# Router pacing, unread matmuls and an earlier weight split in an attention and mixture-of-experts kernel

## The chip, the cores and the metric

The kernel runs on one core of a Trainium2 chip. The metric is the device time of one execution in microseconds. Five engines work side by side, each with its own instruction queue: TensorE (PE, matmuls and transposes), VectorE (DVE), ScalarE (ACT), GpSimd (POOL) and SyncE (SP, which issues most DMA transfers).

## The reference, cut to what matters

```python
# 4 x 8 heads, 512 local tokens (window 32) and 32 global ones, head size 64
x = attention(q_l, k_l, v_l, q_g, k_g, v_g)       # 4 x 544 = 2176 tokens x 512
logits = x @ w_gate                                # 8 experts
order = argsort(-logits.flatten())                 # best pair first
for idx in order:
    tok, e = idx // 8, idx % 8
    if assigned[tok] >= 0 or counts[e] >= 272:
        continue
    assigned[tok] = e; counts[e] += 1
for e in range(8):
    out[assigned == e] = relu(x[assigned == e] @ w1[e]) @ w2[e]
g = out @ w_gate2                                  # gated layer, 512 -> 1536 -> 512
return (silu(g) * (out @ w_val)) @ w_out
```

The capacity of an expert is 272 tokens. A token goes to its best expert that still has room, and the order over all pairs decides who gets the room.

## The kernel before, in words

**Attention** comes first. Beside it a converter (class `Convert`) rewrites the weights of the last, gated layer into a format of 32-bit words: for each half tile it loads raw data (L110), takes a magnitude on ScalarE (L116), builds the word in three VectorE instructions (L122 to L124) and stores it (L128). `LD` says how many rounds a load runs ahead of the magnitude, `RAWB` how many raw buffers there are. Thirty of the 36 half tiles are converted in attention, the last six later, a little at every tick.

**The router** fills the experts one at a time (`Router.phase`). A phase finds the score limit of one expert in six steps: VectorE compares all scores with 32 limits (L678, `cmp`), TensorE counts by 17 short matmuls (L685), VectorE picks the bracket (L688 to L690) and keeps the upper bound (L671 to L674). Then come the number of the expert (`eis`, L704, which SyncE reads to load that expert's weights), the mask, the prefix sum (L717, L718), a one-hot comparison (L734 or L739) with a small product beside it (`h3` at L728, `rh` at L729), and the index matmuls (L743). For expert 0, `W` in these lines is GpSimd, for all others it is VectorE. `Router.after` takes the assigned tokens out (its count matmul is L767).

**The experts** run in four groups of two. Expert k's 272 tokens are gathered by three indirect DMAs (`fetch`, L884), transposed on TensorE (L902) in blocks of 128, 128 and 16, and split into a rounded part `xH` (ScalarE, L904) and a remainder `xL` (VectorE, L905); every product is three matmuls, H by H, H by L and L by H. The weights, in tiles of 512 KB, are split in the same way by `parts` (L983 on ScalarE, L984 on VectorE). `moe` runs h(f), the first layer, and y(f), the second; `gated` runs the gated layer of one expert of the group; four such blocks of expert 0 (`early`) come between expert 0 and expert 1. Banks b0 to b5 are in pairs: `hb` for h, `yb` for y, and gated blocks go round the three pairs.

**The order of the work** is written by one generator, `background`, which hands out the router's instructions step by step. After each piece of 12 matmuls the main program calls `tick`, and a step that yields n is followed by n ticks until the next. While expert k is fetched, a countdown (`GW`, `GL`) runs in the same steps before its transposes are issued. `hurry` changes the yields. `wait_for(k)` drives the generator without any ticks until expert k's transposed tokens are there; in that case the transposes go to the banks b0 to b2, otherwise to one bank, `xbank`. `pump` splits a tile if it was asked for at least `LAG` ticks ago, and at the latest when the product needs it; `load` issues the DMAs of the next tiles.

Of the kernel before, what the change touches and what calls it, by code (L numbers as in the profile page):

```python
# [14 lines left out]
ALU = mybir.AluOpType  # L15
# [49 lines left out]
CV0, CV1 = 3, 6  # L65
QB = 8
PL = 2
RAWB, CB, FB, LD = 5, 3, 4, 3
NC = 30
EN = 36  # L70
UO, LW = 0, 39
# [470 lines left out]
class Router:  # L542
# [110 lines left out]
    def phase(s, n):  # L653
        nc, V, K, b = s.nc, s.nc.vector, s.K, s.bank
# [4 lines left out]
        if not last:  # L659
            lo = s.gmin  # L660
            KS, NR = KN[0]
            cmp, ge = s.cmp[:, :, 0:KS], s.ge[:, 0:KS]
            V.tensor_scalar(s.d, s.hi, s.gmin, 1e-26, op0=ALU.subtract, op1=ALU.max)
            Td = s.Td[:, 0:KS * NR].rearrange("p (r k) -> p r k", k=KS)
            V.tensor_scalar(Td, s.io[0], s.d, None, op0=ALU.mult)
            def step(k):

                return Td[:, k, 1:2]
            def bound(k):

                V.tensor_scalar(s.m1, k1, KS - 1.5, 1e38, op0=ALU.is_ge, op1=ALU.mult)  # L671
                V.tensor_scalar(s.k2, k1, 1.0, None, op0=ALU.add)
                V.scalar_tensor_tensor(s.cd, s.k2, step(k), old, op0=ALU.mult, op1=ALU.add)
                V.scalar_tensor_tensor(s.hi, s.cd, s.m1, s.hi, op0=ALU.max, op1=ALU.min)  # L674
            parts = ((0, 9), (9, NCH)) if n == 0 else ((0, NCH),)
            for k in range(NR):
                for c0, c1 in parts:
                    V.scalar_tensor_tensor(cmp[:, c0:c1], Td[:, k, None, :].to_broadcast([128, c1 - c0, KS]), lo,  # L678
                                           s.v[:, c0:c1, None].to_broadcast([128, c1 - c0, KS]), op0=ALU.add, op1=ALU.is_le)
                if k:  # L680
                    bound(k - 1)
                yield TA, RF
                cnt = b[:, 0:KS]
                for c in range(NCH):
                    nc.tensor.matmul(cnt, s.ohr[:, c].rearrange("p r e -> p (r e)"), cmp[:, c, :], start=c == 0, stop=c == NCH - 1)  # L685

                k1, new = s.k1[k % 2], s.lo2[k % 2]
                V.tensor_scalar(ge, cnt, s.nd, -1.0, op0=ALU.is_ge, op1=ALU.add, accum_out=s.ke)  # L688
                V.tensor_reduce(k1, s.ke.to_broadcast([128, 32]), axis=AX.X, op=ALU.max, apply_transpose=True)
                V.scalar_tensor_tensor(new, k1, step(k), lo, op0=ALU.mult, op1=ALU.add)  # L690
                old, lo = lo, new

            V.scalar_tensor_tensor(s.ew, s.ke, k1, s.w8p, op0=ALU.is_ge, op1=ALU.mult)
            V.tensor_reduce(s.em, s.ew.to_broadcast([128, 32]), axis=AX.X, op=ALU.max, apply_transpose=True)
            bound(NR - 1)
            V.tensor_scalar(s.G, s.v, lo, None, op0=ALU.is_ge)
            V.tensor_scalar(s.A, s.v, s.hi, None, op0=ALU.is_ge)
            V.tensor_tensor(s.G, s.G, s.A, op=ALU.subtract)
        else:
            V.scalar_tensor_tensor(s.e8, s.pen, OUTV / 2, s.w8, op0=ALU.is_ge, op1=ALU.mult)  # L700
            V.tensor_reduce(s.em, s.e8, axis=AX.X, op=ALU.max)
            V.tensor_scalar(s.A, s.v, OUTV / 2, None, op0=ALU.is_ge)
            V.memset(s.G, 0.0)
        V.tensor_scalar(s.eis[n], s.em, -1.0, 8.0, op0=ALU.mult, op1=ALU.add)  # L704
        s.known = n
        yield 1, 0.0

# [8 lines left out]
        p = b[:, 320:354]  # L716
# [5 lines left out]
        W = nc.gpsimd if n == 0 else V  # L722
# [2 lines left out]
            V.tensor_copy(s.lob[:, 0:NCH], s.lo)  # L725
        V.tensor_tensor(s.hb, s.pp[:, None, :].to_broadcast([128, 4, NCH]), s.thr[:, :, None].to_broadcast([128, 4, NCH]), op=ALU.is_ge)
        yield 1, 0.0
        W.tensor_tensor(s.h3, s.hb[:, 0:3], s.hb[:, 1:4], op=ALU.subtract)  # L728
        W.tensor_tensor(s.rh, s.h3.rearrange("p k c -> p c k")[:, :, :, None].to_broadcast([128, NCH, 3, 2]),  # L729
                        s.rid[:, :, None, :].to_broadcast([128, NCH, 3, 2]), op=ALU.mult)  # L730
        for c0, c1 in ((0, 8), (8, NCH + 1)):
# [3 lines left out]
            else:  # L735

                x = slice(c0, min(c1, NCH))
# [36 lines left out]
GW, GL = 6, 12  # L774

EARLY = (4, 5)
CV2 = 0.4
LA0 = 3
MO = 1
# [2 lines left out]
WB, LOOK, RAWS, LAG = 6, 4, 4, 4  # L782
class Ffn:
# [39 lines left out]
    def background(s):  # L823


        pend, now = [], None
        for k in range(E):
            for y in s.steps(k):
                yield s.hurry(k, y)
                if pend and now is None and s.moes >= pend[0] - 1:  # L830
                    now = s.fetch(pend.pop(0))
                    left = next(now)
                    yield 1, 0.0
                elif now is not None:
                    left -= y[0]
                    if left <= 0:
                        x = next(now)
                        if isinstance(x, int):
                            left = x
                        else:  # L840
                            yield x
                            yield from now
                            now = None
            if k < E:
                s.done_phase = k
            pend.append(k)
            if now is None and s.moes >= pend[0] - 1:
                now = s.fetch(pend.pop(0))
                left = next(now)
                yield 1, 0.0  # L850
        while pend or now is not None:
            if now is not None:
                x = left
                while isinstance(x, int):
                    for _ in range(x):
                        yield 1, 0.0
                    x = next(now)
                yield x
                yield from now
                now = None  # L860
            elif s.moes >= pend[0] - 1:
                now = s.fetch(pend.pop(0))
                left = next(now)
            else:
                yield 1, 0.0
# [6 lines left out]
    def hurry(s, k, y):  # L872

        if k == 1:
            return (0 if y[0] == 1 else TA, y[1])

        return (y[0] + (y[0] > 1 and k > 1 and not s.cv.finished), y[1])

    def fetch(s, k):

# [4 lines left out]
                                         in_offset=bass.IndirectOffsetOnAxis(ap=s.R.idx[k][0:n, blk:blk + 1], axis=0))  # L885
        if k == 0:

            yield 2
            for m in range(2):
                s.pump(m, 0)  # L890
                yield (1, 3)[m]
        else:
            yield GW if k == 1 else GL
        xH = s.pool.tile([128, 4, TE], F32R, name="xH", bufs=2)
        xL = s.pool.tile([128, 4, TE], F32R, name="xL", bufs=2)
        s.xT[k] = (xH, xL)
        for blk, n in enumerate((128, 128, 16)):
# [7 lines left out]
            nc.vector.tensor_tensor(xL[:, :, sl], p, xH[:, :, sl].bitcast(F32), op=ALU.subtract)  # L905
            yield 0, 0.0
            if not s.waiting:
                yield 1, 0.0
        s.ready.add(k)

    def convert(s, n):
# [105 lines left out]
    def wait_for(s, k):  # L1017
        s.waiting = True
        while k not in s.ready:
            next(s.bgen)  # L1020
            s.load()
        s.waiting = False

    def moe(s, k, e):
# [144 lines left out]
    def run(s, ext):  # L1169
# [3 lines left out]
        for _ in s.bgen:  # L1173
            if s.R.known == 0:
                while s.nd < LA0:
                    s.dma(s.nd); s.asked[s.nd] = -1; s.nd += 1
            if s.done_phase == 0:
                break
        s.wait_for(0)
# [57 lines left out]
```

## Time and profile before

| | |
|---|---|
| median of 3 runs | 941.58 us (940.79 to 944.29) |
| profiled execution | 935.68 us, span 933.9 us |
| mean granted TensorE clock | 0.959 |
| TensorE busy | 855.0 us (92% of the span) |
| VectorE busy | 598.8 us (64%) |
| ScalarE busy | 398.0 us (43%) |

The span goes from the first to the last instruction of the profiled execution; busy times are sums over the instructions of an engine, and TensorE's are modelled from its pipelined matmuls.

### The profile page before, as it was taken

Reading aid. Unit: us, or ns where it says so; the run is one execution under the profiler, and the core shown is the slowest. Engines: PE = TensorE matmul, PEld = TensorE weight load, DVE = VectorE, ACT = ScalarE, POOL = GpSimd, SP = SyncE. Lnnn points to the kernel's source line nnn. Section 1 sums busy time; section 2 is a strip of 40 time slices with the busy share of each in tenths; the row PEclk is TensorE's granted clock in tenths of the full one; section 3 lists DMA queues with packets and bytes.
Section 4 is the critical chain, followed back from the end, with each engine's and each line's share of the span. In section 5 each row is a group of like instructions: output and inputs, shape, how many; then the busy total and the mean of one; then the engine's idle time right before and its main releaser. Section 6 shows DMA issues by size and latency. Waiting matters only on the chain.

```text
span 933.9 us, 19229 instructions
## 1 busy us (share of the span) xinstructions
PE 855.0 (92%) x7567; PEld 791.7 (85%) x7567; DVE 598.8 (64%) x1486; ACT 398.0 (43%) x827; POOL 111.9 (12%) x189
## 2 busy tenths in 40 slices
PE   6999998638879888999999989999999999999997
PEld 6888887428878887889989888899999889999985
DVE  3688778787889876658888776575545335644410
ACT  4888788313444332324433322245444234443300
POOL 5343321010100000110100100210100020000002
PEclk9999999858989999999999999999999999999999
DMA  7998988242546522434532221365422345522101
GB/s 176 251 268 234 277 261 266 101 160 68 184 157 212 192 73 90 138 102 147 181 116 92 69 71 66 126 215 159 137 91 90 92 137 178 156 72 92 46 1 56
DMA packets 109962, 130.72 MB, mean 140 GB/s; under 512 B 57456, under 2 KB 75120, under 8 KB 109872
## 3 DMA queue, kind: packets, MB, share of 16 engines
q1 hardware_dynamic: 106432, 120.45, 42.1%
q0 software_dynamic: 2896, 8.92, 2.7%
q8 instruction: 59, 0.97, 0.4%
q14 instruction: 31, 0.25, 0.1%
q10 hardware_dynamic: 544, 0.13, 0.1%
HBM read 111.12 MB, written 18.35 MB: 139 GB/s over the span
## 4 chain that ended last, share of the span: by engine, by line
PE 50%; issue 21%; DVE 20%; ACT 4%; DMA 2%; POOL 1%; SPq 0%; POOLq 0%; DVEq 0%; ACTq 0%
PE b L1013 9%; PE b L1015 8%; PE b L1014 8%; DVE wHL L984 4%; PE b L1130 4%; PE b L1131 4%; PE b L1132 4%; DVE r_cmp L678 2%; PE s L303 2%; PE tr L323 2%; PE o L334 2%; DVE b L1078 1%; ACT dH L1079 1%; PE o L339 1%; DMA cv_raw<-moe_w_val 1%
## 5 line engine op out<-in xcount | busy, mean ns | idle before, releaser
L1013 PE MATMUL b<-yH,wHL 128*128 128x272 f32 x768 | 228.7, 298 | 0.0
L1015 PE MATMUL b<-yH,wHL 128*128 128x272 f32 x768 | 224.9, 293 | 0.0
L1014 PE MATMUL b<-yL,wHL 128*128 128x272 f32 x768 | 224.5, 292 | 0.0
L984 DVE TENSOR_TENSOR wHL<-raw,wHL 128x1024 fp32r<-128x1024 f32 x140 | 169.0, 1225 | 45.2 <-ACT wHL L983 44.7
L983 ACT CAST wHL<-raw 128x1024 fp32r<-128x1024 f32 x140 | 143.3, 1047 | 77.9 <-PE b L1132 42.4
L1013 PEld LDWEIGHTS b<-yH,wHL 128*128 128x128 f32 x768 | 148.1, 193 | 3.1 <-issue 3.0
L1014 PEld LDWEIGHTS b<-yL,wHL 128*128 128x128 f32 x768 | 148.6, 194 | 0.2 <-DVE yL L1063 0.2
L1015 PEld LDWEIGHTS b<-yH,wHL 128*128 128x128 f32 x768 | 148.2, 193 | 0.0
L1079 ACT CAST dH<-b 128x272 fp32r<-128x272 f32 x96 | 37.1, 387 | 182.7 <-DVE b L1078 182.7
L1078 DVE TENSOR_TENSOR b<-b,si 128x272 f32<-128x272 f32 x96 | 42.8, 446 | 57.7 <-PE b L1015 57.5
L1013 PE MATMUL b<-dH,wHL 128*128 128x272 f32 x256 | 76.7, 299 | 1.0 <-ACT wHL L983 1.0
L1013 PE MATMUL b<-xH,wHL 128*128 128x272 f32 x252 | 75.3, 299 | 2.2 <-ACT xH L904 1.3
L1015 PE MATMUL b<-dH,wHL 128*128 128x272 f32 x256 | 75.2, 294 | 2.3 <-DVE wHL L984 2.3
L1130 PE MATMUL b<-wHL,dH 128*128 128x512 f32 x192 | 76.3, 397 | 0.0
L1014 PE MATMUL b<-dL,wHL 128*128 128x272 f32 x256 | 74.9, 292 | 1.5 <-DVE dL L1041 1.5
L1131 PE MATMUL b<-wHL,dL 128*128 128x512 f32 x192 | 75.9, 395 | 0.0
L1132 PE MATMUL b<-wHL,dH 128*128 128x512 f32 x192 | 75.9, 395 | 0.0
L1014 PE MATMUL b<-xL,wHL 128*128 128x272 f32 x252 | 73.9, 293 | 0.3 <-DVE xL L905 0.3
L1015 PE MATMUL b<-xH,wHL 128*128 128x272 f32 x252 | 74.0, 294 | 0.0
L1080 DVE TENSOR_TENSOR dL<-b,dH 128x272 fp32r<-128x272 f32 x96 | 42.4, 442 | 43.6 <-ACT dH L1079 43.1
L1040 ACT ACTIVATE dH<-b 128x272 fp32r<-128x272 f32 x64 | 25.5, 398 | 103.7 <-PE b L1015 98.8
L884 POOL DMA_INDIRECT xg<-xd,r_idx x24 | 26.0, 1085 | 264.0 <-DVE b L1078 74.8
(237 smaller groups left out, 1609.5 us busy)
## 6 DMA issues: line engine op xcount, KB each, us to landing
raw<-wd SPq DMA_DIRECT2D x76, 512.0 KB, 3.7
raw<-moe_w SPq DMA_DIRECT2D x64, 512.0 KB, 3.8
wd<-cv_f SPq DMA_DIRECT2D x36, 256.0 KB, 4.8
cv_raw<-moe_w_gate SPq DMA_DIRECT2D x12, 512.0 KB, 6.3
cv_raw<-moe_w_val SPq DMA_DIRECT2D x12, 512.0 KB, 4.4
cv_raw<-moe_w_out SPq DMA_DIRECT2D x12, 512.0 KB, 6.9
xd<-xt SPq DMA_DIRECT2D x16, 256.0 KB, 5.9
st<-k_l SPq DMA_DIRECT2D x28, 128.0 KB, 5.3
```

Source lines behind the costliest of these rows:

```text
L884: nc.gpsimd.indirect_dma_start(out=xg[0:n, blk, :], out_offset=None, in_=s.K.xd[:, :], in_offset=bass.IndirectOffsetOnAxis(ap=s.R.idx[k][0 ...
L983: nc.scalar.copy(w[:, 0], raw)
L984: nc.vector.tensor_tensor(w[:, 1], raw, w[:, 0].bitcast(F32), op=ALU.subtract)
L1013: nc.tensor.matmul(out, wH, xH, start=start, stop=False)
L1014: nc.tensor.matmul(out, wH, xL, start=False, stop=False)
L1015: nc.tensor.matmul(out, wL, xH, start=False, stop=stop)
L1078: nc.vector.tensor_tensor(b, b, si, op=ALU.mult)
L1079: nc.scalar.copy(dH[:, f, :], b)
L1080: nc.vector.tensor_tensor(dL[:, f, :], b, dH[:, f, :].bitcast(F32), op=ALU.subtract)
L1130: nc.tensor.matmul(ob[i], dh, H[:, f % 2, :], start=f == 0, stop=False)
L1131: nc.tensor.matmul(ob[i], dl, H[:, f % 2, :], start=False, stop=False)
L1132: nc.tensor.matmul(ob[i], dh, L[:, f % 2, :], start=False, stop=f == 11)
```

## The change

The converter's loads go one round further ahead, with seven buffers instead of five. The expert number is written before the bounds and masks. `h3` of expert 0 moves from GpSimd to VectorE. Router steps of more than one tick take one tick more for all experts from the third on, also after the converter has ended. A new function `warm` issues matmuls whose result is never read, at four places. The first three weight tiles are split while expert 0's rows are gathered. While TensorE waits for an expert's tokens, their transposes are issued without the countdown; blocks that aren't waited for are two ticks apart instead of one. While expert 0 is waited for, no further loads are issued. The four early blocks stay as they are.

```diff
-RAWB, CB, FB, LD = 5, 3, 4, 3
+RAWB, CB, FB, LD = 7, 3, 4, 4
...
             V.tensor_reduce(s.em, s.ew.to_broadcast([128, 32]), axis=AX.X, op=ALU.max, apply_transpose=True)
+            V.tensor_scalar(s.eis[n], s.em, -1.0, 8.0, op0=ALU.mult, op1=ALU.add)
             bound(NR - 1)
...
-        V.tensor_scalar(s.eis[n], s.em, -1.0, 8.0, op0=ALU.mult, op1=ALU.add)
+            V.tensor_scalar(s.eis[n], s.em, -1.0, 8.0, op0=ALU.mult, op1=ALU.add)
...
-        W.tensor_tensor(s.h3, s.hb[:, 0:3], s.hb[:, 1:4], op=ALU.subtract)
+        V.tensor_tensor(s.h3, s.hb[:, 0:3], s.hb[:, 1:4], op=ALU.subtract)
...
+W0, W1, W2, W3 = 4, 6, 8, 2
...
-                    if left <= 0:
+
+                    if left <= 0 or s.waiting and k > 1:
                         x = next(now)
...
-        return (y[0] + (y[0] > 1 and k > 1 and not s.cv.finished), y[1])
+        return (y[0] + (y[0] > 1 and k > 1), y[1])
+
+    def warm(s, n):
+
+        x = s.R.iota2.rearrange("p w c -> p (w c)")[:, 0:512]
+        for _ in range(n):
+            s.nc.tensor.matmul(s.B[s.hb[1]], s.K.identb, x, start=True, stop=True)
...
+            s.warm(W0)
             yield 2
-            for m in range(2):
-                s.pump(m, 0)
-                yield (1, 3)[m]
+            for m in range(3):
+                s.parts(m); s.np += 1
+                yield 1
+            s.warm(W1)
         else:
+            if s.waiting:
+                s.warm(W2)
             yield GW if k == 1 else GL
+            if s.waiting:
+                s.warm(W3)
...
             if not s.waiting:
-                yield 1, 0.0
+                yield 2, 0.0
         s.ready.add(k)
...
         while k not in s.ready:
             next(s.bgen)
-            s.load()
+            if k:
+
+                s.load()
...
-                    s.dma(s.nd); s.asked[s.nd] = -1; s.nd += 1
+                    s.dma(s.nd); s.asked[s.nd] = -LAG; s.nd += 1
```

## Rows read from the trace of the kernel before

**Rows 1.** The page's view of the span in 40 slices: TensorE's granted clock.

```profile
PEclk9999999858989999999999999999999999999999
```

**Rows 2.** Busy time by stretch: stretch, its length, each engine's busy us, clock, DMA share, GB/s.

```profile
core 0: us, PE busy (x) PEld busy (x) DVE busy (x) ACT busy (x) POOL busy (x), PEclk, DMA share, GB/s
...
176.00:209.00 33.00, 9.96 (x156) 8.16 (x156) 27.85 (x122) 3.47 (x5) 4.55 (x5) 0.53 0.33 113
209.00:249.00 40.00, 33.94 (x301) 32.55 (x297) 32.35 (x105) 12.79 (x20) 2.38 (x2) 0.84 0.35 106
...
302.00:337.00 35.00, 29.77 (x251) 29.42 (x250) 29.49 (x73) 13.04 (x28) 2.77 (x3) 1.00 0.54 172
337.00:377.00 40.00, 34.84 (x325) 33.85 (x325) 28.06 (x94) 13.21 (x27) 0.59 (x1) 0.90 0.18 62
...
418.00:470.00 52.00, 50.09 (x457) 48.69 (x456) 45.90 (x124) 23.38 (x38) 6.01 (x5) 1.00 0.50 155
470.00:515.00 45.00, 42.44 (x425) 41.44 (x425) 36.08 (x108) 16.12 (x35) 0.00 (x0) 1.00 0.31 98
515.00:570.00 55.00, 48.56 (x433) 47.07 (x432) 39.49 (x131) 16.56 (x37) 3.37 (x4) 0.94 0.22 68
...
395.00:400.00 5.00, 5.00 (x23) 3.85 (x23) 2.82 (x11) 0.27 (x2) 0.00 (x0) 1.00 0.30 106
```

**Rows 3.** TensorE's waits, 302 to 570 us: us in total, times, longest.

```profile
PE rbank L685 <- DVE r_cmp L678: 7.9, 5, 3.3
PE xbank L902 <- DVE xL L905: 6.5, 4, 2.4
PE rbank L717 <- DVE r_Mb L712: 3.3, 3, 2.2
PE rbank L767 <- DVE r_acc L759: 2.4, 1, 2.4
```

**Rows 4.** VectorE's groups by line, 302 to 606: busy us, mean ns, idle before.

```profile
L984 DVE TENSOR_TENSOR wHL<-raw,wHL 128x1024 fp32r<-128x1024 f32 x53 | 64.3, 1228 | 9.4 <-ACT wHL L983 8.9 <-issue 0.5
L1078 DVE TENSOR_TENSOR b<-b,si 128x272 f32<-128x272 f32 x44 | 19.5, 443 | 7.9 <-PE b L1015 7.8
L1080 DVE TENSOR_TENSOR dL<-b,dH 128x272 fp32r<-128x272 f32 x44 | 19.4, 442 | 20.0 <-ACT dH L1079 19.5 <-issue 0.5
...
L728 DVE TENSOR_TENSOR r_h<-r_hb 128x51 f32<-128x51 f32 x6 | 1.2, 205 | 0.0
```

**Rows 5.** ScalarE's waits in attention, 0 to 176 us.

```profile
ACT cv_a L116 <- DMA cv_raw<-moe_w_val: 5.6, 4, 2.2
```

**Rows 6.** Timeline, 193 to 220 us: start, us, instruction, idle before it.

```profile
193.98 0.15 DVE L704 TENSOR_SCALAR r_ei<-r_em 128x1 int32<-128x1 f32 x1
...
196.07 0.59 POOL L728 TENSOR_TENSOR r_h<-r_hb 128x51 f32<-128x51 f32 x1 [40.93 <-DVE r_hb L726]
...
205.74 1.97 PE L902 MATMUL b<-identf,xg 128*128 128x128 f32 x8 [5.22 <-DMA xg<-xd,r_idx]
207.91 0.60 PE L902 MATMUL b<-identf,xg 16*128 16x16 f32 x4 [0.21 <-DMA xg<-xd,r_idx]
...
216.97 0.39 PE L1013 MATMUL b<-dH,wHL 128*128 128x272 f32 x1 [0.99 <-ACT wHL L983]
...
219.77 0.59 PE L1015 MATMUL b<-dH,wHL 128*128 128x272 f32 x1 [2.28 <-DVE wHL L984]
```

**Rows 7.** Timeline where the early blocks end and expert 1 begins.

```profile
263.58 2.36 DVE L984 TENSOR_TENSOR wHL<-raw,wHL 128x1024 fp32r<-128x1024 f32 x2 [0.50 <-ACT wHL L983]
...
267.30 0.61 PE L685 MATMUL rbank<-r_cmp,r_ohr 128*128 128x32 bf16 x17 [4.66 <-DVE r_cmp L678]
...
268.06 0.44 DVE L1080 TENSOR_TENSOR dL<-b,dH 128x272 fp32r<-128x272 f32 x1 [0.45 <-ACT dH L1079]
...
269.17 0.59 PE L1013 MATMUL b<-xH,wHL 128*128 128x272 f32 x1 [1.26 <-ACT xH L904]
```

**Rows 8.** Timeline of VectorE: first and last of the nine instructions of a step.

```profile
344.05 0.24 DVE L688 TENSOR_SCALAR_CACHE_REDUCE r_ge<-rbank,r_nd 128x32 bf16<-128x32 f32 x1
...
346.04 0.22 DVE L674 SCALAR_TENSOR_TENSOR r_hi<-r_cd,r_m,r_hi 128x1 f32<-128x1 f32 x1
```

## The prediction

> **What bounds the kernel now.** I read the page's line of TensorE's granted clock over the span first: each digit is a fortieth of the span, 23.3 us, in tenths of full speed, and it falls in four of them between 163 and 280 us [rows 1]. So the question for any edit is where TensorE still stands or runs slowly. The view of busy time by stretch answers it: from 176 to 209 TensorE has 10 us of work in 33 at a clock of 0.53, because VectorE finds the first expert's tokens alone; from 209 to 249 (expert 0) it has 33.9 us in 40 at clock 0.84; from 302 to 377 and 418 to 570 it still loses time in pieces [rows 2].
>
> For the last part, lost time in a stretch is idle time plus (1 - clock) times the stretch: 5.2 us in 302-337, 5.2 + 4.0 in 337-377, 1.9 in 418-470, 2.6 in 470-515, 6.4 + 3.3 in 515-570, in all 28.6 us. The list of waits says for what: the router's counting matmuls waiting for VectorE's comparison (7.9 us), the token transposes waiting for VectorE to empty their one bank (6.5), the prefix-sum matmul (3.3), the count matmul L767 (2.4) [rows 3]. All are VectorE. It isn't full there (28.1 of 40 us in 337-377 [rows 2]), so it is its queue's order that hurts: what the next matmul needs stands behind splits of 1.23 us each [rows 4].
>
> **The change part by part.** Sums are made against the profiled execution, 935.7 us with a span of 933.9. The three timed runs have a median of 941.6, 5.9 us above it; I carry each difference over to that median.
>
> *Attention (RAWB 7, LD 4).* Each converter load is issued one round earlier, with two more buffers; bytes are the same. ScalarE waited for these loads 5.6 us in four places [rows 5], with other engines still at work. Best case all of it and some queueing behind it, -5; worst +1, since the first round puts one more 512 KB load into the queue, ahead of the next heads' loads. I take -2.
>
> *Up to the first expert's matmul.* The expert number is written before seven small instructions instead of after them: it was done at 193.98 and would be about 1.0 us sooner, and the three weight loads with it. h3 leaves GpSimd (0.59 us) for VectorE, where the same shape takes 0.21 [rows 4, 6]: the index matmuls could start about 0.4 us sooner, but VectorE's two large comparisons start 0.2 later. Against that, the third tile's split adds 1.23 us to VectorE's queue ahead of the first comparison and of xL. Ten unread matmuls of 512 columns cost about 0.22 us each at full clock (23 in 5.0 us, last row of [rows 2]), double that at half: 4.3 us at most, in gaps where TensorE stood anyway; the last of these gaps is 5.2 us, until the gathered rows land at 205.7 [rows 6]. If that cover were gone they would cost up to 4.3 us. I take 0, bounds -2.5 and +1.5.
>
> Here a rule of the Trainium skill bears on it ("TensorE: Matmul & The Clock Gate", Part 1: the throttled clock is the resting state, and activity lifts it). The trace agrees: the clock is 0.53 where TensorE has 10 us of work in 33 [rows 2]. By that rule the unread matmuls would let the transposes (2.6 us at half clock [rows 6]) and what follows run at full clock, and the term would be its lower bound of -2.5; I keep 0, since VectorE, late by one split, would take it back.
>
> *Expert 0.* In the kernel before, the third tile was split only when y(0) asked for it: TensorE stood 0.99 and 2.28 us and fell to half clock behind it [rows 6]. Now it is split before the expert starts. The stretch 209-249 loses 6.1 us idle and 6.4 to the clock; but VectorE has 32.4 us of work in it [rows 2], all of it still to do, so at most 40 - 32.4 = 7.6 can go. I take -5, bounds -7.5 and -2. The skipped load() calls while waiting for expert 0 cost nothing: SyncE has no other transfer between those loads.
>
> *Early blocks and the boundary to expert 1.* By a count of the program's ticks, the countdown of the second fetch is already spent when the early blocks end, so the new "waiting and k > 1" condition fires where the old one did: the transposes keep their place in the queue. Two things do change. One split fewer stands in VectorE's queue at the boundary, where two took from 263.58 to 265.94 [rows 7]: -1.2. And two unread matmuls go ahead of the transposes, into bank hb[1]. The fourth early block uses that same bank, and its last reader is dL L1080, which ended at 268.50 [rows 7]. So twelve transposes, which stood ahead of the router matmul of 267.30 and ran beside VectorE's backlog, now wait for that backlog's end. Before, expert 1 started 0.67 us behind this dL (269.17); now follow 0.9 us of unread matmuls, 2.6 us of transposes at the slow clock (1.97 + 0.60 for the first expert's [rows 6]) and the last copy, about 4 us: +3.3. Expert 1 then starts with a warmer clock, -1. Together +1, bounds -2 and +3.5.
>
> A second rule speaks against this part of the change ("TensorE: Matmul & The Clock Gate", Part 2: matmuls stay in program order, only weight loads are pulled ahead). The trace agrees: expert 1's first matmul stands behind a router matmul that waits 4.66 us [rows 7].
>
> *Group 0 and group 1: router paced.* Steps of more than one tick now take one more, also after the converter is done; it ends at about tick 50, in the middle of group 0. A tick is 12 matmuls of about 0.12 us (29.8 us for 251 in 302-337, at full clock [rows 2]), some 1.5 us. One router step is nine VectorE instructions from 344.05 to 346.26, 2.2 us [rows 8]. A gated block adds b, dL and the hole between them (0.44 + 0.44 + 20.0/44 = 1.34 us in two ticks [rows 4]), and splits, two in eight ticks, 0.3 us a tick. Before, a step every two ticks: 1.1 + 0.67 + 0.3 = 2.1 us of VectorE in 1.5 of TensorE; after, every three: 1.7 in 1.5, and six ticks without steps while the transposes go through, two ticks apart instead of one, so that the copies of a block have 3 us. Three pairs of banks cover a lag of some 6 us. So most waits of [rows 3] should go, with the clock's dips behind them, but not L767's 2.4, which comes before the pacing differs. Group 0 (14.4 of the 28.6 us): -10, bounds -4 and -13. Group 1 and its experts (14.2): -7, bounds -3 and -10.
>
> *What is late next.* By the same count, expert 3's tokens are known two ticks into expert 2 instead of ten ticks ahead of it, and its fetch countdown has not run out when expert 2 ends: its three transposes come in the gap. Their banks are those whose yL is written last, then copies follow, some 3.3 us until the first two matmuls can go; 2.2 of these are transposes and a router step that TensorE had to do anyway. Expert 5 is caught with its smallest block alone. And the sixth phase now runs beside experts 4 and 5, which had no router work. I take +1.5 + 0.5 + 0.5 = +2.5, bounds 0 and +8 (expert 3 as bad as expert 1).
>
> The sum: -2 + 0 - 5 + 1 - 10 - 7 + 2.5 = **-20.5**, a profiled time of 915 and a median of **921 us**.
>
> **The rivals.** *Half of it:* VectorE stays the limit in the groups with 1.7 us per tick against 1.5, so pacing gives half (-8.5 for -17), and the load lead gives nothing: 0 + 0 - 5 + 1 - 8.5 + 2.5 = -10, 932 us. For it: the figure of 1.7; against: VectorE's 12 us of idle time in 337-377.
>
> *All of it:* attention -4, first matmul -2, expert 0 -7, boundary -1, groups -23, late parts +3: -34, 908 us. For it: every wait named is one of order; against: VectorE's 32.4 us in expert 0.
>
> *Slower:* VectorE's lag is not removed but carried to the boundaries. The groups then give nothing, and experts 3 and 5 each wait as expert 1 did, 4.66 us for the comparison and 1.26 for the copies [rows 7], with some 2 us of slow clock after it, about 8 us each: -2 + 0 - 5 + 1 + 0 + 16 = +10, 952 us. It decides once the two waits take over 6 us more than the groups give. For it: expert 3's fetch is surely late; against: its rows have 12 ticks, 18 us, to land, and router work in expert 2 falls.
>
> *The named part does nothing:* the condition for the second expert's transposes has no effect. That is part of my forecast.
>
> **How the numbers follow.** Two runs of this kernel tell about 0.5% apart, 4.7 us. Forecast 0.55, half of it 0.20, all of it 0.16, slower 0.09. The likeliest has its own range of 913 to 930; from "all of it" to a little over "half of it" the range is 907 to 937. Faster by over 0.5%: all of the first and third, 0.71, and most of "half of it", 0.13, makes 0.84; within 0.5%: 0.09, the rest of "half of it" and 0.02 of the slower case; slower: 0.07.
>
> **What would show it.** Right: no idle time of over 1 us before y(0) of expert 0; the waits of router matmuls and xbank transposes in groups 0 and 1 under 6 us together; clock at or near 1.00 there. At expert 1 the unread matmuls start only when dL has ended, and the transposes behind them. At expert 3 the transposes write banks b, not xbank. Wrong: attention ending more than 3 us later, expert 3 or 5 waiting over 5 us, or the lost time of 302 to 570 still above 20 us.

## The result and the profile after

The changed kernel takes 907.98 us (median of 4 runs, 906.74 to 909.42) where the kernel before takes 941.18 (4 runs): ratio 0.9647, 95% interval 0.9612 to 0.9681, or 33 us less. The forecast was 921, the range 907 to 937. The sign held, and the range held by 1 us; the gain is 13 us larger than forecast, at the end that the rival "all of it" had given (908).

The profiled execution of the changed kernel took 909.42 us with a span of 907.6. Line numbers have moved by up to 18 (L984 is now L1000, L902 is L918, L1013 to L1015 are L1029 to L1031, L1080 is L1098; the unread matmul is L887).

First the page's line of TensorE's granted clock, which answers to [rows 1]:

```profile
PEclk9999999857889999999999999999999999999999
```

The dips between 160 and 270 us are still there and no shallower. What has gone is idle time after 300 us, with the smaller dips behind it (0.90 and 0.94 in [rows 2]). The view of busy time by stretch, for stretches as in [rows 2] (its columns are the same):

```profile
177.00:211.00 34.00, 14.84 (x159) 9.63 (x159) 29.21 (x123) 4.37 (x6) 4.64 (x4) 0.52 0.35 112
211.00:249.00 38.00, 34.00 (x320) 32.95 (x317) 34.08 (x108) 13.69 (x22) 3.85 (x3) 0.85 0.44 151
302.00:337.00 35.00, 33.03 (x278) 32.79 (x278) 28.98 (x72) 13.77 (x28) 2.76 (x3) 1.00 0.52 166
337.00:372.00 35.00, 34.69 (x328) 33.18 (x328) 26.72 (x73) 15.66 (x32) 1.20 (x2) 1.00 0.32 105
371.00:429.00 58.00, 58.00 (x385) 51.05 (x384) 38.16 (x97) 18.84 (x28) 10.95 (x12) 1.00 0.45 146
429.00:459.00 30.00, 29.27 (x294) 28.25 (x293) 25.95 (x78) 13.62 (x24) 0.00 (x0) 1.00 0.48 147
459.00:514.00 55.00, 55.00 (x508) 54.45 (x506) 41.70 (x107) 22.56 (x47) 3.38 (x3) 1.00 0.29 95
514.00:560.00 46.00, 45.87 (x324) 40.78 (x321) 29.76 (x91) 12.57 (x23) 4.90 (x5) 1.00 0.32 105
```

From 302 to 560 us the clock is 1.00 everywhere, and TensorE is idle 2.0 us in the first of these stretches, 0.7 at expert 3's start (429 to 459) and 0.4 in the others together. Its waits from 285 to 570 us, which answer to [rows 3] and begin 17 us earlier:

```profile
PE rbank L768 <- DVE r_acc L760: 2.0, 1, 2.0
PE b L1030 <- DVE dL L1059: 1.5, 1, 1.5
PE b L1029 <- DVE xL L921: 0.7, 1, 0.7
PE rbank L685 <- DVE r_cmp L678: 0.5, 2, 0.3
```

The waits for the comparison, the transposes' bank and the prefix sum, 17.7 us in [rows 3], have become 0.5 (0.2 from 302 us on). VectorE's instructions have not become shorter (groups by line, 302 to 606 us, as [rows 4]): the hole ahead of dL is still 20.0 us.

```profile
L1000 DVE TENSOR_TENSOR wHL<-raw,wHL 128x1024 fp32r<-128x1024 f32 x62 | 74.4, 1220 | 7.6 <-ACT wHL L999 7.5
...
L1098 DVE TENSOR_TENSOR dL<-b,dH 128x272 fp32r<-128x272 f32 x44 | 19.4, 442 | 20.0 <-ACT dH L1097 20.0
```

The timeline of TensorE up to expert 0's second layer, as [rows 6]:

```profile
200.28 1.87 PE L887 MATMUL b<-r_iota,identb 128*128 128x512 bf16 x4
...
202.02 2.72 PE L887 MATMUL b<-r_iota,identb 128*128 128x512 bf16 x6
206.23 1.11 PE L918 MATMUL b<-identf,xg 128*128 128x128 f32 x4 [1.49 <-DMA xg<-xd,r_idx]
208.97 1.66 PE L918 MATMUL b<-identf,xg 128*128 128x128 f32 x8 [1.63 <-DMA xg<-xd,r_idx]
...
211.22 2.16 PE L1054 MATMUL b<-xH,wHL 128*128 128x272 f32 x8
...
218.66 0.37 PE L1029 MATMUL b<-dH,wHL 128*128 128x272 f32 x1
```

The two stalls at y(0) (0.99 and 2.28 us before) are gone. The ten unread matmuls ran at half clock and left the stretch at 0.52; the first eight matmuls of the expert take 2.16 us. The boundary to expert 1, as [rows 7]:

```profile
265.81 0.44 DVE L1098 TENSOR_TENSOR dL<-b,dH 128x272 fp32r<-128x272 f32 x1 [0.45 <-ACT dH L1097]
266.30 1.01 PE L887 MATMUL b<-r_iota,identb 128*128 128x512 bf16 x2 [6.00 <-DVE dL L1098]
...
267.11 2.44 PE L918 MATMUL b<-identf,xg 128*128 128x128 f32 x12
...
269.49 0.63 PE L685 MATMUL rbank<-r_cmp,r_ohr 128*128 128x32 bf16 x17
...
269.96 0.55 PE L1029 MATMUL b<-xH,wHL 128*128 128x272 f32 x1
```

This is the order that was forecast: the unread matmuls wait for the last reader of bank hb[1], the transposes wait behind them, and expert 1 begins 3.7 us behind the end of that dL, where it had been 0.67. Of the four places with unread matmuls three come into play here: ten run ahead of expert 0, two ahead of expert 1's transposes and two ahead of expert 3's; the eight of `W2` don't run.

### The profile page after: what moved, and what is told of

Its sections match the earlier page's. It is cut to its first block, busy times and chain, and to the rows that moved or that the text cites. A ratio compares the mean times of both kernels' runs of the same rounds, so it can differ in the third digit from the quotient of the medians.

```text
span 907.6 us, 19267 instructions
## 1 busy us (share of the span) xinstructions
PE 852.1 (94%) x7581; PEld 786.3 (87%) x7581; DVE 598.7 (66%) x1487; ACT 397.8 (44%) x827; POOL 113.2 (12%) x188
## 3 DMA queue, kind: packets, MB, share of 16 engines
q1 hardware_dynamic: 106432, 120.45, 42.8%
## 4 chain that ended last, share of the span: by engine, by line
PE 60%; issue 20%; DVE 13%; DMA 3%; ACT 2%; SPq 1%; POOL 1%; POOLq 0%; DVEq 0%; ACTq 0%
PE b L1029 12%; PE b L1030 11%; PE b L1031 11%; PE b L1148 4%; PE b L1149 4%; PE b L1150 4%; PE s L303 3%; DVE wHL L1000 3%; DMA wd<-cv_f 2%; PE tr L323 2%; PE o L334 2%; PE rbank L685 1%; DVE r_cmp L678 1%; PE o L339 1%; PE tr L358 1%
## 5 line engine op out<-in xcount | busy, mean ns | idle before, releaser
L1029 PE MATMUL b<-yH,wHL 128*128 128x272 f32 x768 | 224.9, 293 | 0.0
L1031 PE MATMUL b<-yH,wHL 128*128 128x272 f32 x768 | 221.9, 289 | 0.0
L1030 PE MATMUL b<-yL,wHL 128*128 128x272 f32 x768 | 221.2, 288 | 0.0
L1000 DVE TENSOR_TENSOR wHL<-raw,wHL 128x1024 fp32r<-128x1024 f32 x140 | 168.3, 1221 | 38.3 <-ACT wHL L999 38.2
L1029 PEld LDWEIGHTS b<-yH,wHL 128*128 128x128 f32 x768 | 145.0, 189 | 2.5 <-issue 2.4
L1030 PEld LDWEIGHTS b<-yL,wHL 128*128 128x128 f32 x768 | 145.5, 189 | 0.0
L1031 PEld LDWEIGHTS b<-yH,wHL 128*128 128x128 f32 x768 | 145.0, 189 | 0.0
L1029 PE MATMUL b<-dH,wHL 128*128 128x272 f32 x256 | 77.0, 301 | 0.0
L1031 PE MATMUL b<-dH,wHL 128*128 128x272 f32 x256 | 75.7, 296 | 0.0
L1029 PE MATMUL b<-xH,wHL 128*128 128x272 f32 x252 | 74.7, 296 | 0.7 <-DVE xL L921 0.7
L1096 DVE TENSOR_TENSOR b<-b,si 128x272 f32<-128x272 f32 x96 | 42.8, 445 | 46.6 <-PE b L1031 44.6
L1031 PE MATMUL b<-xH,wHL 128*128 128x272 f32 x252 | 73.0, 290 | 0.0
L1098 DVE TENSOR_TENSOR dL<-b,dH 128x272 fp32r<-128x272 f32 x96 | 42.4, 442 | 43.6 <-ACT dH L1097 43.6
L1058 ACT ACTIVATE dH<-b 128x272 fp32r<-128x272 f32 x64 | 25.5, 398 | 102.3 <-PE b L1031 97.2
## 6 DMA issues: line engine op xcount, KB each, us to landing
st<-k_l SPq DMA_DIRECT2D x28, 128.0 KB, 5.4
```

What stands on the lines that cost most here:

```text
L1000: nc.vector.tensor_tensor(w[:, 1], raw, w[:, 0].bitcast(F32), op=ALU.subtract)
L1029: nc.tensor.matmul(out, wH, xH, start=start, stop=False)
L1030: nc.tensor.matmul(out, wH, xL, start=False, stop=False)
L1031: nc.tensor.matmul(out, wL, xH, start=False, stop=stop)
L1096: nc.vector.tensor_tensor(b, b, si, op=ALU.mult)
L1098: nc.vector.tensor_tensor(dL[:, f, :], b, dH[:, f, :].bitcast(F32), op=ALU.subtract)
```

## The experiments

Times are medians of four runs; the kernel before, run beside them, took 940.1 to 941.2 us, and the ratios are to it, with their 95% intervals. Beside the times I use one mark of the traces, the start of the last yH instruction of each expert (L1062, now L1080; yH is the rounded part of the expert's output): the time from one to the next is the length of a stage, in which a delay from the stages ahead no longer counts.

**Pacing by itself.** Three kernels on top of the kernel before, nothing else changed: the step's extra tick, the two ticks between transposed blocks, and both with the countdown's condition.

```diff
 e1, e3
-        return (y[0] + (y[0] > 1 and k > 1 and not s.cv.finished), y[1])
+        return (y[0] + (y[0] > 1 and k > 1), y[1])
 e2, e3
-                yield 1, 0.0
+                yield 2, 0.0
 e3
-                    if left <= 0:
+                    if left <= 0 or s.waiting and k > 1:
```

> The kernel before with one line of the change: router steps of more than one tick take one more also after the converter is done; the transposes' blocks stay one tick apart. Theory (router steps overfill VectorE's queue, pacing frees it): the waits of L685 and L717 from 302 us to the end of group 1 go from 11.2 us to under 2; the xbank waits (6.5 us) fall by half, since the queue is shorter when they come; lost time there from 28.6 to under 8 us; expert 3 isn't ready in time, and without the new condition its countdown runs on with router steps while TensorE stands, 2 to 8 us; in all 12 to 24 us faster. Rival (the blocks' spacing did it): the waits of the router matmuls stay above 6 us and the gain is under 8 us.

> The kernel before with the transposes' blocks two ticks apart and nothing else. Theory: only the xbank waits go, 6.5 us and the slow clock behind two of them, 1.7 us each, and six ticks without router steps per fetch let VectorE catch up a little: 5 to 12 us faster; L685 and L717 keep most of their 11.2 us. Rival (spacing of the blocks is what counts): over 18 us faster.

> The kernel before with the three edits to the order of the work: one more tick, blocks two ticks apart, transposes at once where TensorE waits. Theory (all of the gain is pacing; load lead, early expert number, h3, third split and unread matmuls give nothing together): within 0.6% of the changed kernel, ratio 0.959 to 0.971 to the kernel before. Rival (the other edits gave some 6 us, as the prediction's first four terms said): ratio 0.970 or more, since those terms are missing.

Measured: 917.84 us (ratio 0.9754, 0.9722 to 0.9785), 925.71 (0.9844, 0.9812 to 0.9876) and 914.65 (0.9734, 0.9702 to 0.9766): 22.3, 14.4 and 25.5 us less than before. TensorE's waits from 300 to 570 us in e1, and then in e2:

```profile
PE rbank L767 <- DVE r_acc L759: 2.0, 1, 2.0
...
PE rbank L685 <- DVE r_cmp L678: 1.2, 2, 0.7
PE xbank L902 <- DVE xL L905: 0.7, 2, 0.5
```

```profile
PE rbank L685 <- DVE r_cmp L678: 6.0, 6, 1.8
PE rbank L767 <- DVE r_acc L759: 2.0, 1, 2.0
PE xbank L902 <- DVE xL L905: 1.9, 2, 1.0
PE rbank L717 <- DVE r_Mb L712: 1.6, 1, 1.6
```

Spacing the steps ends both kinds of wait, though it leaves the transposed blocks as close together as they were; spacing the blocks ends most of the bank's. The two share one queue, so their gains overlap: 36.7 us by themselves, 25.5 together. e1 came as expected; e2 gained more than the 5 to 12 us expected of it and less than its rival's 18. For e3 the rival held: it takes 6.7 us more than the changed kernel, so the other edits are worth about that much together. Pacing carries 25.5 of the 33 us.

**The condition taken out of the changed kernel.**

```diff
-                    if left <= 0 or s.waiting and k > 1:
+                    if left <= 0:
```

> The changed kernel with the countdown's new condition taken out again (the transposes come when the countdown has run out, also while TensorE waits). My prediction's rival, that the condition does nothing, holds at expert 1: the order of its transposes is the same, and 0 us is expected there. At expert 3 the condition puts two unread matmuls and the transposes ahead of two router steps. If it is needed there, those two steps (34 counting matmuls and the VectorE comparison and bracket between them) now stand ahead of the transposes in a gap in which TensorE has nothing else: the last yH of expert 3 would come about 5 us (3 to 8) later after that of expert 2 than the changed kernel's 29.9 us, and the whole takes 911 to 915. If the two steps only change places with work that has to be done anyway, the same gap and 907 to 909.

Measured: 909.56 us (0.9658, 0.9619 to 0.9697), not to be told from 907.98 by the time. The order at expert 1 is the same; at expert 3 it isn't (timeline of TensorE):

```profile
432.40 0.58 PE L685 MATMUL rbank<-r_cmp,r_ohr 128*128 128x32 bf16 x17 [2.01 <-DVE r_cmp L678]
433.04 0.38 PE L887 MATMUL b<-r_iota,identb 128*128 128x512 bf16 x1
433.25 1.38 PE L918 MATMUL b<-identf,xg 128*128 128x128 f32 x12
...
436.61 0.39 PE L1029 MATMUL b<-xH,wHL 128*128 128x272 f32 x1 [1.39 <-DVE xL L921]
```

The transposes stand behind two router steps, with a wait of 2.01 us for the second comparison. From expert 2 to expert 3 it is 32.5 us instead of 29.9; the 2.6 us are just under the 3 to 8 expected, and up to expert 6 2.1 of them are left. So the condition does nothing where its description puts it, at the second expert, and something at the fourth.

**The two unread matmuls ahead of waiting transposes.** Once without them, once written into the other bank.

```diff
 e4
-W0, W1, W2, W3 = 4, 6, 8, 2
+W0, W1, W2, W3 = 4, 6, 8, 0
 e10
-                s.warm(W3)
+                s.warm(W3, s.xb)
```

> The changed kernel without the two unread matmuls ahead of late transposes. Theory (in bank hb[1] they hold the transposes until dL of the fourth early block has ended): expert 1's transposes start right after the early block, some 6 us sooner, and its first matmul comes 2 to 3 us sooner after that dL (before 1.1 us behind its start, changed 4.2); in all 1.5 to 3 us faster than the changed kernel. Rival (the clock that they save is worth as much): no difference, expert 1's first matmuls slower by as much.

> The changed kernel with the two unread matmuls ahead of the waiting transposes written into the bank of the transposes that are not waited for, instead of the bank that the last early block still reads. If their price of 1.8 us (run without them) is the wait for that bank's reader, they now start at about 260.3, as soon as TensorE is there, the transposes follow at once, and the kernel takes 905.5 to 907, expert 1 starting at the same distance from the end of expert 0 as without them. If the price is the matmuls' own time or TensorE's clock, nothing changes: 907 to 909.

Measured: 906.19 us without (0.9637, 0.9606 to 0.9667) and 908.4 in the other bank (0.9639, 0.9581 to 0.9696). The times can't tell them apart; the traces can. Without them, the transposes go through beside VectorE's backlog and expert 1 starts sooner:

```profile
260.07 1.38 PE L918 MATMUL b<-identf,xg 128*128 128x128 f32 x12
264.98 0.62 PE L685 MATMUL rbank<-r_cmp,r_ohr 128*128 128x32 bf16 x17 [3.53 <-DVE r_cmp L678]
266.86 0.60 PE L1029 MATMUL b<-xH,wHL 128*128 128x272 f32 x1 [1.26 <-ACT xH L920]
```

and in the other bank they don't wait either:

```profile
262.59 0.38 PE L887 MATMUL xbank<-r_iota,identb 128*128 128x512 bf16 x1
262.80 1.38 PE L918 MATMUL b<-identf,xg 128*128 128x128 f32 x12
```

From expert 0 to expert 1 it takes 53.2 us in the changed kernel, 51.9 without them and 52.0 in the other bank: it was the bank's reader, not the matmuls' own 0.9 us. What the wait costs has to be read between traces in which expert 0 itself took equally long, since a short stage of expert 0 goes with a long one behind it. Where expert 0 took 34.1 to 34.3 us, the next stage is 55.1 and 55.0 us with the wait (e5 and e9, further kernels with the same code there) and 51.9 and 52.0 without it (e4, e10). Where it took 36.9 to 37.6, the stage is 53.2 and 53.2 with it (the changed kernel, e6) and 50.2 without (e11). The price is 3.0 us in both. The stage after that gives back a third to a half: 128.0 and 128.1 against 129.0 and 129.1 us in the first set, 127.5 and 127.5 against 129.0 in the second. That leaves 1.5 to 2 us, and the medians with and without are 1.8 apart. What is given back is mostly clock. Behind L768's wait, e4 has 0.94 (columns as in [rows 2]) where the changed kernel has 1.00 in its 315 to 330 us:

```profile
311.90:326.90 15.00, 12.48 (x108) 12.30 (x107) 12.18 (x33) 5.19 (x11) 2.76 (x3) 0.94 0.47 144
```

That wait is 2.5 us in e4, e10 and e11, whose clock over the whole stage is 0.99, and 2.5 us in e5 and e9 too, whose clock is 1.00, as the changed kernel's is behind 2.0 us.

**The unread matmuls beside the first gather taken out.**

```diff
-W0, W1, W2, W3 = 4, 6, 8, 2
+W0, W1, W2, W3 = 0, 0, 8, 2
```

> The changed kernel without the ten unread matmuls ahead of expert 0 (the two ahead of late transposes stay). Theory (they end 1.5 us before the gathered rows land, TensorE stands again, and the first eight matmuls of expert 0 take 2.16 us with them as they did in the kernel before): no difference, within 1.5 us of the changed kernel. Rival (the skill's clock rule, without them the clock comes up later): 2.5 us or more slower, and the granted clock between the first matmul of expert 0 and y(0) lower.

Measured: 909.08 us (0.9653, 0.9611 to 0.9695), no difference. Its transposes and first matmuls, to be laid beside those of the changed kernel above:

```profile
210.59 1.12 PE L918 MATMUL b<-identf,xg 128*128 128x128 f32 x4 [4.11 <-DMA xg<-xd,r_idx]
213.38 1.65 PE L918 MATMUL b<-identf,xg 128*128 128x128 f32 x8 [1.68 <-DMA xg<-xd,r_idx]
...
215.50 2.16 PE L1054 MATMUL b<-xH,wHL 128*128 128x272 f32 x8
```

1.12, 1.65 and 2.16 us against 1.11, 1.66 and 2.16: the matmuls that nobody reads bought no clock here.

**The converter's lead, the third tile, and the number with h3, each put back.**

```diff
 e6
-RAWB, CB, FB, LD = 7, 3, 4, 4
+RAWB, CB, FB, LD = 5, 3, 4, 3
 e7
-            for m in range(3):
-                s.parts(m); s.np += 1
-                yield 1
+            for m in range(2):
+                s.pump(m, 0)
+                yield (1, 3)[m]
...
-            if k:
-
-                s.load()
+            s.load()
...
-                    s.dma(s.nd); s.asked[s.nd] = -LAG; s.nd += 1
+                    s.dma(s.nd); s.asked[s.nd] = -1; s.nd += 1
 e8
-            V.tensor_scalar(s.eis[n], s.em, -1.0, 8.0, op0=ALU.mult, op1=ALU.add)
...
-            V.tensor_scalar(s.eis[n], s.em, -1.0, 8.0, op0=ALU.mult, op1=ALU.add)
+        V.tensor_scalar(s.eis[n], s.em, -1.0, 8.0, op0=ALU.mult, op1=ALU.add)
...
-        V.tensor_tensor(s.h3, s.hb[:, 0:3], s.hb[:, 1:4], op=ALU.subtract)
+        W.tensor_tensor(s.h3, s.hb[:, 0:3], s.hb[:, 1:4], op=ALU.subtract)
```

> The changed kernel with RAWB 5 and LD 3 again. Theory (ScalarE's wait for the raw load only became VectorE's wait for a free store buffer, FB 4): ScalarE waits for raw loads 5 to 9 us again, VectorE's waits for stores fall from 5.6 us to 2 to 3, and the time stays within 2 us of the changed kernel. Rival (the prediction's -2 and more): 2 to 4 us slower, attention ending as much later.

> The changed kernel with the third tile split at y(0) again (two tiles through pump while the rows are gathered, asked at -1, and load() while waiting for expert 0). Theory (the prediction's -5: TensorE stood 3.3 us and lost some 2 us of clock): the wait at y(0) and the slow matmuls behind it are back, 3 to 6 us slower than the changed kernel. Rival (VectorE bounds expert 0, so that the wait saved comes back before expert 1): within 1.5 us of the changed kernel, the last yH of expert 0 at the same distance from its first matmul.

> The changed kernel with the expert number written after the bounds and masks again, and h3 of expert 0 on GpSimd again. Theory (the weight loads go out 0.9 us sooner and run into the gather, whose second issue took 1.92 us instead of 0.95 and whose last rows landed 10 us after the index matmuls instead of 9): no difference, within 1.5 us, the gather's second issue back under 1.1 us. Rival (the prediction's terms): 1 to 2 us slower, everything after the router's last step later by that.

Measured: 912.56 us (0.9702, 0.9663 to 0.9741), 911.8 (0.9702, 0.9661 to 0.9742) and 908.46 (0.9655, 0.9617 to 0.9693), or 4.6, 3.8 and 0.5 us more than the changed kernel. The third tile's gain shows in its stage: from the first matmul of expert 0 to its last yH, the four traces of kernels without any of the changes ahead of expert 1 (before, e1 to e3) take 40.1, 39.2, 38.6 and 38.6 us and e7 39.7, but the changed kernel 37.0 and the other traces with the new split 34.1 to 37.6. Their spread goes with the clock: over the last 18 us of expert 0 it is 1.00 in e4, e5, e9 and e10 (34.1 to 34.3 us), over the last 21 us 0.84 in the changed kernel, e6, e11 and e12 (36.9 to 37.6). For e8 the theory held: the gather's second issue is back at 0.95 us, and the time is the same.

The lead's gain does not show so clearly. The last matmuls of attention (L370) start at 175.4, 181.7, 177.5, 178.8 and 179.7 us in the five traces with the old lead (before, e1, e2, e3, e6), mean 178.6, and at 174.9 to 181.1 in the nine with the new one (e11, below, with other numbers of buffers), mean 177.8. In e6 that mark is 2.9 us later than in the changed kernel, and every stage behind it is the same to 0.1 us. The kind of load wait that [rows 5] shows, 5.2 to 9.0 us in the five traces with the old lead, has gone, at most 0.3 us in the nine; VectorE's wait for a free store buffer, 1.8 to 4.5 us in the five, has grown to 5.2 to 8.9 in the eight that keep four buffers (VectorE, 0 to 178 us, changed kernel; before it was 3.3 us, 3 times):

```profile
DVE cv_f L122 <- DMA wd<-cv_f: 5.6, 5, 2.6
```

So one wait was exchanged for another, as the theory for e6 had it, but its time fits neither expectation: 4.6 us is more than the 2 us of the theory and the 2 to 4 of the rival. Put back one at a time, the lead, the third tile, the number with h3 and the ten unread matmuls cost 4.6, 3.8, 0.5 and 1.1 us, and taking out the other two unread ones gains 1.8: 8.2 us in all, beside the 6.7 that e3 lacks. The last three are within the scatter of the runs.

**More buffers for those stores.** Without the two unread matmuls, and with six store buffers for one raw buffer less.

```diff
-RAWB, CB, FB, LD = 7, 3, 4, 4
+RAWB, CB, FB, LD = 6, 3, 6, 4
...
-W0, W1, W2, W3 = 4, 6, 8, 2
+W0, W1, W2, W3 = 4, 6, 8, 0
```

> A version meant to be faster than both: no unread matmuls ahead of the waiting transposes, and six buffers instead of four for the converter's words on their way to memory, paid for with one raw buffer (six instead of seven). If the wait for those stores, 5.6 us on VectorE in the changed kernel's attention, is on the path, it falls under 2 us and attention ends 1 to 3 us sooner: 902 to 905. If it is hidden beside the other engines, or if the sixth raw buffer was needed, 905.5 to 908, as without the unread matmuls alone (906.2).

Measured: 907.09 us (0.9648, 0.9606 to 0.969). The wait for the stores is no longer in the list, and the time is that of e4 within the scatter. The wait was hidden beside the other engines, or the raw buffer given up for it cost as much; this run doesn't separate the two. None of these kernels is measurably faster than the changed one.

**Pacing further.**

```diff
-        return (y[0] + (y[0] > 1 and k > 1), y[1])
+        return (y[0] + (y[0] > 1 and k > 1) + (y[0] > 1 and 1 < k < 5), y[1])
```

> The changed kernel with router steps of more than one tick given two more ticks instead of one in the phases of experts 2, 3 and 4. This tests my slower rival, that spacing carries the lag to the boundaries between experts. In the changed kernel the waits of 296 to 560 us are 4.4 us, nearly all at one count matmul and at expert 3's start, so spacing further has at most 1 us left to give. If tokens that come later are then waited for, expert 3's start, and perhaps that of expert 2, is late by the steps that still stand ahead of it: 912 to 925, with a wait of over 5 us at a boundary. If the phases still end in time, 906 to 909.

Measured: 926.55 us (0.9834, 0.9792 to 0.9877), 18.6 more than with one tick and just above the 912 to 925 expected, but without the wait of over 5 us that was to go with it. TensorE at the boundary to expert 3:

```profile
431.56 0.35 PE L744 MATMUL rbank<-r_rh,r_ol 128*128 128x6 bf16 x8 [2.09 <-DVE r_ol L740]
...
433.46 3.55 PE L887 MATMUL b<-r_iota,identb 128*128 128x512 bf16 x9 [0.24 <-issue]
437.83 0.66 PE L918 MATMUL b<-identf,xg 128*128 128x128 f32 x4 [0.82 <-DMA xg<-xd,r_idx]
...
441.71 0.39 PE L1029 MATMUL b<-xH,wHL 128*128 128x272 f32 x1 [1.27 <-ACT wHL L999]
```

Here the eight of `W2` run too. When expert 2 is done, the index matmuls, the gather, the transposes and the copies of expert 3 are all still to come. From expert 2 to expert 3 it takes 42.8 us, 12.9 more. This is the mechanism of my slower rival, and no single wait shows it: the longest is 2.09 us. TensorE is idle 8.0 us in this stage instead of 0.7, in a chain of steps that should have run beside expert 2, and the granted clock is 0.88 instead of 1.00, 5.1 us: 12.4 of the 12.9.

## Why the prediction held, and which term was too small

By stages, predicted against measured. For the stages up to expert 1 the measured value is a difference of means over the traces with and without the edits (single traces of the same code differ by up to 6 us there); behind it, single traces agree to 0.6 us where the code is the same, and it is the changed kernel's minus the kernel before's.

| stage | predicted | measured |
|---|---|---|
| attention | -2 | -0.8 (178.6 to 177.8) |
| up to expert 0's first matmul | 0 | +0.7 (34.0 in 4 traces, 34.6 in 7) |
| expert 0 | -5 | -3.4 (39.1 in 4 traces, 35.7 in 9) |
| early blocks, boundary to expert 1 | +1 | -0.2 (54.0 in 4 traces, 53.8 in 6) |
| experts 1 to 3 (group 0, expert 3's start) | -10 + 1.5 | -15.8 (173.2 to 157.4) |
| experts 3 to 5 (group 1, expert 5's start) | -7 + 0.5 | -13.7 (179.3 to 165.6) |
| experts 5 to 7 | +0.5 | +2.5 (156.7 to 159.2) |
| sum | -20.5 | -30.7 (timed: -33.2) |

*The step that failed is a size: the pacing term of groups 0 and 1.* The mechanism was right: the waits named in the prediction went, with the clock's dips behind them, and L768's stayed (2.0 of 2.4 us). But I let 17 of 28.6 us go, because I held VectorE to be overfull with 1.7 us of work in a tick of 1.5. That figure joined the highest rate of each kind of work: a router step every three ticks, for instance. In the changed kernel's stretch of 337 to 372 us there are six comparisons in 23 ticks, about one in four, since phases pause between steps; VectorE's 26.72 us busy and its 5.0 us of holes ahead of dL come to 1.36 us a tick. That is under 1.5, and so nothing is left waiting. The trace of before said the same: 28.1 us busy in 40 [rows 2], which I had read and set aside as the argument against "half of it" only. With everything but L767's wait and 1 us at a boundary gone, the two groups would have been some -25, and the median about 913.

The rest of the sum can be found too. From expert 1's mark to expert 5's, TensorE's idle time went from 21.3 to 3.1 us. The clock was 0.97 up to expert 3's mark and 0.98 from there, and is 1.00 in both now: some 8.8 us, of which 1.2 lay between 377 and 418 us (clock 0.97), a stretch that is in none of my terms. Together that is 27 of the 29.5 us in the table. The other 2.5 are work that moved out of these stages, and they stand in the table again as the +2.5 of experts 5 to 7: the router's matmuls take 1.8 us there instead of 0.1 and the transposes 3.2 instead of 2.1, while TensorE is idle 0.5 us instead of 0.3. So the two groups really gave 27, and the sixth phase beside the last experts cost next to nothing by lateness; I had put +0.5 for that.

*Expert 3's start* cost less than the 1.5 us I gave it: in the changed kernel its transposes (429.16, 1.67 us) run at full clock right behind the last matmul, and its first matmul waits 0.7 us. The extra 3.4 us from expert 2 to expert 3 are mostly work that had stood in the stage ahead of it: 85 router matmuls instead of 35, and 12 transposes instead of none.

*Expert 1's boundary* went as forecast. The bank's wait costs 3.0 us from expert 0 to expert 1, where I had put 3.3, and the next stage gives back 1.0 to 1.5. Expert 1 does start with a warmer clock: its matmuls of 272 columns take 0.29 us from the third on, while in e4 the first dozen take 0.40 to 0.60. The rule that matmuls stay in program order (the Trainium skill, "TensorE: Matmul & The Clock Gate", Part 2) is what the trace shows: twelve transposes that were ready (in e4 they go at once) stood 6.00 us behind two matmuls whose result nobody reads.

*Up to expert 0's first matmul* the +0.7 us fits a cost that the prediction had named, the third tile's split in VectorE's queue ahead of the first comparison. In e10 the transposes end 1.2 us sooner behind attention's mark than in the changed kernel, and the router matmul ahead of expert 0 then waits for that comparison (in e12 too, 1.57 us):

```profile
211.39 1.22 DVE L1000 TENSOR_TENSOR wHL<-raw,wHL 128x1024 fp32r<-128x1024 f32 x1
...
213.12 0.78 DVE L678 SCALAR_TENSOR_TENSOR r_cmp<-r_Td,r_gmin,r_v 128x544 bf16<-128x544 f32 x1
...
213.96 0.61 PE L685 MATMUL rbank<-r_cmp,r_ohr 128*128 128x32 bf16 x17 [1.47 <-DVE r_cmp L678]
```

In e7, which splits that tile later, the first matmul comes 34.1 us behind attention's mark; in the seven traces with the split ahead it is 34.6.

*Unread matmuls up to expert 0.* I kept 0 against -2.5 for the right result with a doubtful reason. By the rule of the Trainium skill ("TensorE: Matmul & The Clock Gate", Part 1) activity lifts the clock, and I drew from it that the transposes behind ten matmuls would run at full clock. They took 1.11 and 1.66 us with them, 1.12 and 1.65 without. Here the measurement decides against what I drew from the rule: nothing was gained that VectorE could have taken back.

*Expert 0 and attention* lie within their bounds. For attention the time of e6 (+4.6) and the marks (0.8 on the mean, with a spread of 6) don't agree on the size; what the lead is worth stays open between 0 and some 5 us.

*The rivals.* "Half of it" fell with the figure of 1.7. "All of it" came out at its time with its mechanism, though its terms for the first matmul and expert 0 were too high and its groups (-23) still too small: that its 908 was met is in part luck, since these errors cancel, and so is that the range, which ends at that rival, held by 1 us. "Slower" didn't happen, but one tick more brings its mechanism (e12, still 14 us faster than before). "The named part does nothing" held at expert 1 and not at expert 3, where e9 lacks 2.6 us.

## What to carry to other kernels

Where an in-order engine makes another wait although it is far from full, add up its busy time over the whole stretch and not at the highest rate of each kind of work: if the sum is well under the stretch, spreading the small steps can take nearly all of the wait away. The spacing is bounded on the other side by the boundary at which the steps' result is needed; look there first, since lateness shows as a chain of ordinary instructions with short waits, in the wrong place, and not as one long wait. A filler instruction needs a buffer that nobody still reads, or it holds everything behind it.

## What was not expected of the hardware

- Ten unread matmuls of 512 columns in 4.5 us ran at about 0.45 us each, and the granted clock from 210 to 214 us was still 0.50, the lower of the two levels, 1.2 GHz. In e7, the same ten were followed by four transposes in 0.66 us behind a gap of 1.39, against 1.11 us behind a gap of 1.49 in the changed kernel; behind the next gap, of 2.05 us, the first eight matmuls took 2.16 us again. So the same burst was followed by the higher level in one run and not in the other; what decided it these runs leave open.
- The same attention code ended at 175.4 to 181.7 us in five traces. The profiled execution of before, on which the forecast stood, was the shortest of them, 3.2 us below their mean; its time was 5.9 us below the median.
- A gather's issue on GpSimd took longer when a split of VectorE was running as it began. The changed kernel's timeline:

```profile
201.68 1.18 POOL L894 DMA_INDIRECT xg<-xd,r_idx  x1 [2.73 <-DVE r_eq L756]
203.04 1.23 DVE L1000 TENSOR_TENSOR wHL<-raw,wHL 128x1024 fp32r<-128x1024 f32 x1 [0.26 <-ACT wHL L999]
203.17 1.92 POOL L894 DMA_INDIRECT xg<-xd,r_idx  x1 [0.30 <-issue]
205.39 0.86 POOL L894 DMA_INDIRECT xg<-xd,r_idx  x1 [0.30 <-issue]
```

  The second issue begins with 1.10 us of the split still to run and takes 0.97 longer than the 0.95 of the kernel before, where the split began behind the issue. In the fourteen traces 85 issues, of all experts, begin with more than 0.1 us of a split still to run; undisturbed ones take 0.97, 0.95 and 0.86 us as first, second and third of a gather (expert 0's first 1.18 to 1.20 in every trace). Of the 85, 84 are longer by what was left less 0.11 to 0.13 us: the issue seems to stand until the split is done. The exception is in e8, where the split had begun only 0.02 us ahead of the issue, which took 0.95. The split reads two operands from SBUF. 37 issues that begin while VectorE runs an instruction that reads one of its operands from a matmul's bank (L1096 or L1098, for instance), with 0.15 to 0.42 us left, take 0.85 to 0.98; a short one with two operands in SBUF (L761, 0.21 us left) lengthened none either. The Trainium skill ("GPSIMD Engine Reference", Key points) says that GpSimd shares its SBUF interfaces with VectorE and contends with instructions that have two inputs there. The splits fit that, though no run here was made for it. The held gather isn't what delays the first matmul of expert 0: in e10, where no issue was held, it comes 34.5 us behind attention's mark, against 34.3 to 34.5 in the changed kernel, e4, e6 and e9, where the second was.
